# A fused attention and mixture-of-experts kernel: block sums copied into six chunks by DMA instead of VectorE, a third buffer for the values of the sparse part, full-width summary scores, and two more x tiles transposed by DMA

## The chip, the core and the metric

The kernel runs on one core of a Trainium2 chip. The core has five engines that run their own instruction streams in order: TensorE (PE; its weight loads are shown as PEld), VectorE (DVE), ScalarE (ACT), GpSimd (POOL) and SyncE (SP). They meet through semaphores. TensorE writes its results into PSUM banks; everything else lives in SBUF. Transfers are issued by SP and POOL here, each into a queue of its own, and are carried out by the core's 16 DMA engines.

The metric is the device time of one execution in microseconds, the median of several runs. Before the change it is 668.06 us (three runs: 668.44, 667.29, 668.06).

## What is computed

The first part is a sparse attention over q, k, v of shape (4 batches, 8 heads, 768 positions, 64). Each query sees its neighbours closer than 16 positions, and besides them 24 summaries: for each block of 32 positions the maximum of its keys and the mean of its values.

```python
k_sum = k.reshape(B, H, nb, block, D).max(axis=3)
v_sum = v.reshape(B, H, nb, block, D).mean(axis=3)
mask_l = np.abs(pos[:, None] - pos[None, :]) < window
scores_s = scale * np.einsum('bhsd,bhnd->bhsn', q, k_sum) + np.log(block)
a = softmax(concat([where(mask_l, scale * q @ k.T, -1e9), scores_s]))
out = a @ concat([v, v_sum])          # (B, H, S, D)
```

The second part takes that output as x, 3072 tokens of width 512, computes a routing matrix P (3072 by 8) by an exponential and eight rounds of dividing by row and column sums, and adds up eight experts, each `P[:, e] * (relu(x @ w1[e]) @ w2[e])` with a hidden width of 1024.

## The kernel before

**Pairs.** Attention works on 16 pairs of heads, pair `i` holding heads 2(i%4) and 2(i%4)+1 of batch i//4. Pairs 0 to 3 (batch 0) go through `pair_half`, in halves of 384 positions, and start the kernel. Pairs 4 to 15 go through `pair_whole`, six chunks of 128 positions each; the change is about these twelve.

**The steps of a pair from 4 on**, with their names in the planner's table `U`: POOL issues the loads of k, q (two transfers each, L282) and v (L287). TensorE transposes k and q (`tr`, L301; pairs 12 to 15 by DMA on SP instead, L328) and copies go to `kT`, `qT`. VectorE takes the block maxima of k (`ks`, L333) and spreads them by head into `ksT` (`km`, L339). TensorE sums the blocks of v with a constant matrix (`vs`, L355) into PSUM; VectorE scales that into chunk 0 of a value tile `V_e` (L361) and copies it into chunks 1 to 5 (L365); both are the unit `Vs`. SP (pairs 4 to 11) or POOL (12 to 15) copies the rows of v that a chunk's neighbours need into the other half of the partitions of `V_e` (`near`, four small transfers, L375 and L377). TensorE makes the scores in two blocks (`S`, L345), ACT the exponentials, VectorE the masks (L410) and the edge parts in `E_e` (`ed`, L418 and L422). `summaries_2` (`ss`, L459) makes the scores against the summaries, the first half of the positions into PSUM partitions 0 to 63 and the second half into 64 to 127, each with a weight tile of 64 columns; ACT's exponentials of them go into `E_e` (L470). `values` (`A`, L433 and L439) multiplies by v and, with a second group of matmuls, by `V_e`. VectorE normalizes (L540, L541). Last, x is transposed into `xT`: by TensorE into PSUM and a copy (`to_xT`, L548), and for pairs 12 to 14 by a DMA transpose on SP (`x_dma`, L558), as `X_BY_DMA = 12` says; pair 15 goes by TensorE.

**Buffers.** There are `NE = 2` tiles each of `E_e` and `V_e`. So the block sums and the neighbours of pair i wait for the values of pair i-2. POOL writes the constant parts of these tiles once (`value_constants` L694 to L697, `edge_constants` L690), between the load of w2 of expert 0 and the loads of pair 5. There are six buffers for k, q and v.

**The order of the work.** A small list planner (`Plan`) runs when the kernel is built. Each unit has an engine, a cost, dependences, a priority and, for transfers, a lag until the data are taken as landed; the planner picks the earliest startable unit of each engine and so writes each engine's instruction order. On the chip that order is fixed: an engine waits at an instruction until its semaphores are there, whatever stands ready behind it.

**What fills TensorE.** Expert 0 is computed without routing weights, in eight halves of 384 tokens (`hidden0` L209 and `project0` L214), and is slotted between the attention steps as soon as a batch's x is there. Experts 1 to 7 follow; their two products are done by a seven-multiplication scheme on two-by-two blocks (L762, L813). They need their weights, all of x and P.

Of the kernel before, what the change touches and what calls it, by code (L numbers as in the profile page):

```python
# [10 lines left out]
BF16 = mybir.dt.bfloat16  # L11
# [117 lines left out]
def kernel(  # L129
# [30 lines left out]
    BY_DMA = 12  # L160
    X_BY_DMA = 12
    WHOLE = 12
# [56 lines left out]
    NB = PB  # L219
    NE = 2  # L220
    NS = 1
    NA = 3
    stage = ExitStack()
    with tc.manual_schedule():
# [14 lines left out]
        ks = [attn.tile([128, 1, 32], BF16, name=f"ks{i}") for i in range(NB)]  # L239
        ksT = [attn.tile([128, 128], BF16, name=f"ksT{i}") for i in range(NB)]  # L240
        v_x = [attn.tile([128, 2, G, VD], BF16, name=f"vx{i}") for i in range(NQ)]
# [3 lines left out]

        E_e = [attn.tile([128, G, 128], BF16, name=f"Ee{i}") for i in range(NE)]
        V_e = [attn.tile([128, G, 2 * VD], BF16, name=f"Ve{i}") for i in range(NE)]

# [88 lines left out]
        def key_max_split(i):  # L337
            r = i % NB
            nc.vector.tensor_tensor(out=ksT[r][:, 0:64].rearrange("p (j n) -> p j n", j=2),  # L339
                                    in0=ks[r][:].to_broadcast([128, 2, 32]),  # L340
                                    in1=own[:].to_broadcast([128, 2, 32]), op=ALU.mult)
# [16 lines left out]
        def block_out(i):  # L358
            vs = at.pop(("vs", i))[0:64, :].rearrange("p (j d) -> p j d", j=2)
            dst = V_s[i][0:64, :] if i < PB else V_e[i % NE][0:64, 0, :]  # L360
            nc.vector.tensor_tensor(out=dst.rearrange("p (j x) -> p j x", j=2)[:, :, 0:D], in0=vs,  # L361
                                    in1=own_n[:].to_broadcast([64, 2, D]), op=ALU.mult)
            if i >= PB:
                ve = V_e[i % NE]
                nc.vector.tensor_copy(out=ve[0:64, 1:G, :],  # L365
                                      in_=ve[0:64, 0:1, :].to_broadcast([64, G - 1, 2 * VD]))


        def near_values(i):

            sv, ve = v_x[i % NQ], V_e[i % NE]
            eng = nc.sync if i < BY_DMA else nc.gpsimd
            for j in range(2):
                c0, q0 = VD * j, 64 + 32 * j
                eng.dma_start(out=ve[q0 + W:q0 + 2 * W, 1:G, c0:c0 + VD],  # L375
                              in_=sv[128 - W:128, j, 0:G - 1, :])
                eng.dma_start(out=ve[q0:q0 + W, 0:G - 1, c0:c0 + VD],  # L377
                              in_=sv[0:W, j, 1:G, :])
# [48 lines left out]
        def values(i, h):  # L427
            sv, ee, ve, em = v_x[i % NQ], E_e[i % NE], V_e[i % NE], at["em", i]
            av = at["av", i, h] = bank("a", "av")
            for cc in range(HG):  # L430
                c, o = HG * h + cc, cc * 2 * VD
                for j in range(2):
                    nc.tensor.matmul(av[:, o + j * VD:o + (j + 1) * VD],  # L433
                                     lhsT=em[:, j, c, :], rhs=sv[:, j, c, :],
                                     start=(cc == 0 and j == 0), stop=False,
                                     skip_group_check=True)
            for cc in range(HG):
                c, o = HG * h + cc, cc * 2 * VD
                nc.tensor.matmul(av[:, o:o + 2 * VD], lhsT=ee[:, c, :], rhs=ve[:, c, :],  # L439
                                 start=False, stop=True, skip_group_check=True)  # L440

        def summaries(i, h, tag):
            r = i % NB
            ss, rhs = bank(tag, "ss"), qT[r][:, W + h * HS:W + (h + 1) * HS]
            wait_busy("s", i, h, ss)
            at["ss", i, h] = ss
            if i < PB and not h:
                for j in range(2):
                    p = slice(64 * j, 64 * j + 64)
                    nc.tensor.matmul(ss[32 * j:32 * j + 32, 0:HS], lhsT=ks[r][p, 0, :], rhs=rhs[p],  # L450
                                     start=True, stop=True)
                return
            nc.tensor.matmul(ss[:, 0:HS], lhsT=ksT[r][:], rhs=rhs, start=True, stop=True)

        def summaries_2(i):
            r, ss = i % NB, bank("a", "ss")
            for h in range(2):
                at["ss", i, h] = ss[64 * h:64 * h + 64]
                nc.tensor.matmul(ss[64 * h:64 * h + 64, 0:HS], lhsT=ksT[r][:, 0:64],  # L459
                                 rhs=qT[r][:, W + h * HS:W + (h + 1) * HS], start=True, stop=True)  # L460

# [189 lines left out]
        def constants():  # L651
# [10 lines left out]
            for t in ksT:  # L662
                nc.vector.memset(t[:, 64:128], 0.0)
            for t, n in ((own, 64), (own_n, 32)):
# [214 lines left out]
        def pair_start(i, prio):  # L879
# [18 lines left out]
            if i >= PB:  # L898
                U["km", i] = add("DVE", 0.23, lambda: key_max_split(i), [U["ks", i]] + war_q[2:], prio)
            buf = Buffer("a")  # L900
            U["vs", i] = add("PE", 0.4, lambda: block_sums(i),
                             [U["v", i]] + ([U.get(("A", i - NE, 1)), U["vc", i % NE]] if i >= PB else []), prio + 0.01, opens=[buf])
            sc = add("DVE", 0.25, lambda: summary_constants(i), [], prio - 1.0) if 0 < i < PB else None
            U["Vs", i] = add("DVE", 0.28 if i < PB else 0.7, lambda: block_out(i), [U["vs", i], sc],
                             prio + 0.01, uses=[buf])
# [36 lines left out]
        def pair_whole(i, prio):  # L942
            U["near", i] = add("SP" if i < BY_DMA else "POOL", 2.4 if i < BY_DMA else 3.0, lambda: near_values(i),
                               [U["v", i], U.get(("A", i - NE, 1)), U["vc", i % NE]], prio, lag=5.0 if i < BY_DMA else 3.5)
            x1 = []
# [14 lines left out]
            for h in range(2):  # L960
# [4 lines left out]
            buf = Buffer("a")  # L965
            U["ss", i, 0] = U["ss", i, 1] = add("PE", 0.22, lambda: summaries_2(i),
                                                [U["km", i], U["kT", i, 1], U.get(("A", i - NE, 1))], prio, opens=[buf])
            for h in range(2):
                U["sx", i, h] = add("ACT", 0.46, lambda h=h: summary_exp(i, h), [U["ss", i, h]], prio, uses=[buf])
            for h in range(2):  # L970
                buf = Buffer("a")
                U["A", i, h] = add("PE", 0.4, lambda h=h: values(i, h),
                                   [U["mk", i, h], U["ed", i], U["sx", i, h], U["Vs", i], U["near", i]],
                                   prio, opens=[buf])
# [76 lines left out]
        load_pair(PB, "kqv")  # L1051
        load("w2", lambda: load_w2(0), 0.85, 4.0)
        for n in range(NE):
            U["vc", n] = last[0] = add("POOL", 1.2, lambda n=n: value_constants(n), [last[0]])
            U["ec", n] = last[0] = add("POOL", 0.7, lambda n=n: edge_constants(n), [last[0]])
# [36 lines left out]
        def transposed():  # L1092
# [4 lines left out]
            if X_BY_DMA < NP:  # L1097
                nc.gpsimd.tensor_copy(out=warm[:, 4:5], in_=xT[0:32, PB - 2, (B - 1) * S:(B - 1) * S + 1])
            ve = V_e[(NP - 1) % NE]
            for j in range(2):  # L1100
                nc.gpsimd.tensor_copy(out=warm[:, 2 + j:3 + j],
                                      in_=ve[64 + 32 * j:96 + 32 * j, G - 2, VD * j:VD * j + 1])

        last[0] = add("POOL", 0.3, transposed, [last[0], U["near", NP - 1]] + [U["kT", NP - 1, z] for z in range(2)]
                      + [U["x", i] for i in range(X_BY_DMA, NP - 1)])
# [211 lines left out]
```

## Time and profile before

| quantity | value |
|---|---|
| median of three runs | 668.06 us |
| the profiled execution, its own time | 668.44 us |
| its span, first to last instruction | 666.7 us |
| TensorE, VectorE, ScalarE, GpSimd busy | 657.9, 549.2, 410.5, 198.3 us |
| moved by DMA | 67.89 MB in 112,542 packets |
| expert 0's first product with w2 | 34.77 us |
| values of pairs 4, 5, 6, 7, 8, 9 start on TensorE | 40.5, 49.9, 57.2, 63.1, 69.8, 76.5 us |
| values of pairs 10 to 15 start | 83.3, 88.7, 99.3, 105.1, 111.3, 115.4 us |
| first product of expert 1 | 129.47 us |
| last matmuls of expert 0 | about 165 us |

Busy time of each engine by stage, in us of the stage's length:

| stage (us) | PE | DVE | ACT | POOL | GB/s |
|---|---|---|---|---|---|
| 34 to 50 | 15.23 of 16 | 13.30 | 9.76 | 15.50 | 149 |
| 50 to 66 | 16.00 | 15.15 | 11.55 | 15.82 | 145 |
| 66 to 82 | 16.00 | 14.71 | 12.01 | 11.14 | 131 |
| 82 to 98 | 16.00 | 13.39 | 9.95 | 4.27 | 105 |
| 98 to 118 | 20.00 of 20 | 15.42 | 13.32 | 5.67 | 36 |
| 118 to 166 | 48.00 of 48 | 41.47 | 27.51 | 1.18 | 45 |

The table says where each engine is busy, not which one holds up the others. TensorE is busy throughout from 35 us on, and since its ends are modelled, "busy" alone doesn't say that it streams without gaps; for that one looks at the starts of successive matmuls and at the list of its waits.

### The profile page before, as it was taken

Reading aid. Unit: us, or ns where it says so; the run is one execution under the profiler, and the core shown is the slowest. Engines: PE = TensorE matmul, PEld = TensorE weight load, DVE = VectorE, ACT = ScalarE, POOL = GpSimd, SP = SyncE. Lnnn points to the kernel's source line nnn. Section 1 sums busy time; section 2 is a strip of 40 time slices with the busy share of each in tenths; the row PEclk is TensorE's granted clock in tenths of the full one; section 3 lists DMA queues with packets and bytes.
Section 4 is the critical chain, followed back from the end, with each engine's and each line's share of the span. In section 5 each row is a group of like instructions: output and inputs, shape, how many; then the busy total and the mean of one; then the engine's idle time right before and its main releaser. Section 6 shows DMA issues by size and latency. Waiting matters only on the chain.

```text
span 666.7 us, 13260 instructions
## 1 busy us (share of the span) xinstructions
PE 657.9 (99%) x5132; PEld 434.0 (65%) x5132; DVE 549.2 (82%) x1035; ACT 410.5 (62%) x768; POOL 198.3 (30%) x256
## 2 busy tenths in 40 slices
PE   8999999999999999999999999999999999999996
PEld 4656665555676666666666666666666666666665
DVE  7889978799989787888789887888778877988776
ACT  6767766555986566556565665656665656556652
POOL 8899622100132222222221222222122213222123
PEclk9999999999999999999999999999999999999999
DMA  9999992700863647473654656373837465334656
GB/s 168 165 149 145 132 88 43 127 0 1 137 112 64 117 75 116 79 127 64 98 102 76 123 83 106 65 127 61 130 64 130 77 95 95 64 64 112 159 134 198
DMA packets 112542, 67.89 MB, mean 102 GB/s; under 512 B 77920, under 2 KB 90464, under 8 KB 112480
## 3 DMA queue, kind: packets, MB, share of 16 engines
q0 software_dynamic: 94800, 57.46, 65.7%
q1 hardware_dynamic: 17152, 9.58, 6.5%
q8 instruction: 40, 0.66, 0.4%
q14 instruction: 22, 0.18, 0.1%
q10 hardware_dynamic: 528, 0.02, 0.0%
HBM read 52.45 MB, written 6.29 MB: 88 GB/s over the span
## 4 chain that ended last, share of the span: by engine, by line
PE 94%; DMA 3%; POOL 2%; issue 0%; DVE 0%; ACT 0%; POOLq 0%; DVEq 0%
PE yps L813 22%; PE pA L762 22%; PE pY L813 17%; PE pQ L762 11%; PE yps L214 6%; PE hps L209 6%; PE pR L762 5%; DMA w<-in_moe_w_dram 3%; PE sg L345 1%; PE tkq L301 1%; PE av L433 1%; PE vs L355 1%; PE av L439 1%; POOL vx L287 1%; PE tx L548 1%; PE ss L459 1%
## 5 line engine op out<-in xcount | busy, mean ns | idle before, releaser
L813 PEld LDWEIGHTS <-h 128*128 128x128 f16 x2352 | 230.1, 98 | 89.3 <-issue 1.0
L841 POOL DMA_DIRECT2D out_acc<-y x120 | 101.5, 880 | 372.0 <-ACT y L837 97.8
L837 ACT ACTIVATE y<-pY,P_sb 128x256 f32<-128x256 f32 x168 | 79.8, 476 | 124.2 <-PE pY L813 122.5
L828 DVE SCALAR_TENSOR_TENSOR out_acc<-yps,P_sb,out_acc 128x512 f32<-128x512 f32 x128 | 95.2, 744 | 30.2 <-PE yps L813 30.0
L796 DVE TENSOR_TENSOR h<-h 128x1024 f16<-128x1024 f16 x168 | 109.0, 684 | 1.2
L813 PE MATMUL pY<-w,h 128*128 128x256 f16 x672 | 100.2, 273 | 0.6 <-ACT y L837 0.6
L762 PE MATMUL pA<-xT,w 128*128 128x512 f16 x336 | 98.5, 379 | 0.0
L813 PE MATMUL yps<-w2sum,h 128*128 128x256 f16 x672 | 98.1, 273 | 0.0
L813 PE MATMUL yps<-w,h 128*128 128x256 f16 x672 | 93.3, 273 | 0.0
L828 DVE SCALAR_TENSOR_TENSOR out_acc<-pY,P_sb,out_acc 128x512 f32<-128x512 f32 x84 | 62.9, 748 | 29.9 <-PE pY L813 28.2
L762 PEld LDWEIGHTS <-w 128*128 128x128 f16 x672 | 65.8, 98 | 30.9 <-issue 0.2
L762 PEld LDWEIGHTS <-w1sum 128*128 128x128 f16 x504 | 49.3, 98 | 44.2
L784 DVE CUSTOM_DVE_ANT_0 h<-pQ,snap 128x512 f16<-128x512 f32 x84 | 57.6, 685 | 6.0 <-ACT snap L205 3.3
L784 DVE CUSTOM_DVE_ANT_0 h<-pA,snap 128x512 f16<-128x512 f32 x84 | 57.3, 683 | 6.0 <-PE pA L762 5.9
L200 ACT ACTIVATE h<-pA 128x512 f16<-128x512 f32 x84 | 50.6, 603 | 12.4 <-PE pA L762 12.2
L200 ACT ACTIVATE h<-pR 128x512 f16<-128x512 f32 x84 | 50.1, 596 | 7.5 <-PE pR L762 7.4
L205 ACT COPY pR<-pA 128x512 f32<-128x512 f32 x84 | 48.0, 571 | 7.4 <-PE pA L762 6.4
L813 PE MATMUL pY<-w2sum,h 128*128 128x256 f16 x336 | 50.4, 273 | 0.0
L762 PE MATMUL pA<-xsum,w 128*128 128x512 f16 x168 | 50.0, 379 | 0.0
L762 PE MATMUL pQ<-xsum,w1sum 128*128 128x512 f16 x168 | 50.0, 379 | 0.0
L762 PE MATMUL pQ<-xT,w1sum 128*128 128x512 f16 x168 | 50.0, 379 | 0.0
L762 PE MATMUL pA<-xsum,w1sum 128*128 128x512 f16 x168 | 50.0, 379 | 0.0
(149 smaller groups left out, 845.9 us busy)
## 6 DMA issues: line engine op xcount, KB each, us to landing
out_acc<-y POOLq DMA_DIRECT2D x120, 256.0 KB, 3.4
w<-in_moe_w_dram POOLq DMA_DIRECT2D x15, 1024.0 KB, 10.6
out_dram<-out_acc SPq DMA_DIRECT2D x24, 256.0 KB, 2.5
qst<-in_q_dram POOLq DMA_DIRECT2D x32, 96.0 KB, 5.8
vx<-in_v_dram POOLq DMA_DIRECT2D x15, 192.0 KB, 6.6
kst<-in_k_dram POOLq DMA_DIRECT2D x24, 96.0 KB, 6.0
w<-in_moe_w_dram POOLq DMA_DIRECT2D x4, 256.0 KB, 7.9
kst<-in_k_dram POOLq DMA_DIRECT2D x3, 192.0 KB, 4.7
```

Of the source, the lines that this page charges most:

```text
L200: nc.scalar.activation(out=out, in_=in_, func=AF.Relu, bias=0.0, scale=1.0)
L205: (nc.scalar.copy if eng == "ACT" else nc.vector.tensor_copy)(out=out, in_=in_)
L209: nc.tensor.matmul(hp[:, 0:n], lhsT=w1s[e][:, dk, f * 128:(f + 1) * 128], rhs=xT[:, dk, t0:t0 + n], start=(dk == 0), stop=(dk == KD - 1))
L214: nc.tensor.matmul(yp[:, d], lhsT=h[:, f, c * 128:(c + 1) * 128], rhs=w2s[e][:, f, d], start=(f == 0), stop=(f == KF - 1))
L287: nc.gpsimd.dma_start(out=v_x[i % NQ][:].rearrange("p j g x -> p (j g) x")[:, :, 0:D], in_=v[b, h0:h0 + 2].rearrange("j (g p) d -> p (j g) ...
L762: nc.tensor.matmul(dst[:], lhsT=lhsT, rhs=rhs, start=first and k == 0, stop=k == HK - 1, skip_group_check=True)
L784: nc.vector._custom_dve(dve_ops.TENSOR_ADD_SAT, out=ring(e, p, q)[:, q % 2, blk, :], in0=at[src, e, p, q][:], in1=at.pop(("snap", n, e, p, ...
L796: nc.vector.tensor_tensor(out=h[:, :, out_, :], in0=h[:, :, a, :], in1=h[:, :, b, :], op=op)
L813: nc.tensor.matmul(dst[:, d], lhsT=lhsT, rhs=rhs, start=f == 0 and n in (1, 5, 2), stop=f == HF - 1, skip_group_check=True)
L828: nc.vector.scalar_tensor_tensor(out=o, in0=y, scalar=scalar, in1=o, op0=ALU.mult, op1=ALU.add)
L837: nc.scalar.activation(out=at[key][:, d], in_=src, func=AF.Copy, bias=0.0, scale=P_sb[:, t, e:e + 1])
L841: nc.gpsimd.dma_start(out=o, in_=at.pop(("y", e, p, c, key))[:], accum_op=ALU.add)
```

## The change

- `X_BY_DMA` goes from 12 to 9: the x tiles of pairs 9 and 10 are transposed by DMA on SP, too (pair 11 is the last of its batch and stays with TensorE).
- `V_e` gets `NV = 3` tiles in place of two, and POOL writes the constants of three. Block sums and neighbours of pair i now wait for the values of pair i-3. `E_e` stays at two.
- The copy of the block sums into chunks 1 to 5 moves from VectorE to a DMA with a repeated source (`spread_sums`), on SP for pairs 4 to 11 and on POOL for 12 to 15, right behind the four transfers of `near`. `values` depends on it (`U["sp", i]`).
- `ksT` is 192 columns wide, with the 64 columns of the summaries in the middle and zeros around them. `summaries_2` takes a window of 128 columns that starts at 64 or at 0, so each of its two matmuls has full width, and the second one adds to the first in PSUM.
- The planner gets other costs for the units touched, so it writes other orders for all engines between about 37 and 220 us. The order of TensorE up to the summary scores of pair 4 is as before.

```diff
-    X_BY_DMA = 12
+    X_BY_DMA = 9
+    NV = 3
-        ksT = [attn.tile([128, 128], BF16, name=f"ksT{i}") for i in range(NB)]
+        ksT = [attn.tile([128, 192], BF16, name=f"ksT{i}") for i in range(NB)]
-        V_e = [attn.tile([128, G, 2 * VD], BF16, name=f"Ve{i}") for i in range(NE)]
+        V_e = [attn.tile([128, G, 2 * VD], BF16, name=f"Ve{i}") for i in range(NV)]
...
         def block_out(i):
...
-            if i >= PB:
-                ve = V_e[i % NE]
-                nc.vector.tensor_copy(out=ve[0:64, 1:G, :],
-                                      in_=ve[0:64, 0:1, :].to_broadcast([64, G - 1, 2 * VD]))
+        def spread_sums(i):
+            ve = V_e[i % NV]
+            (nc.sync if i < BY_DMA else nc.gpsimd).dma_start(
+                out=ve[0:64, 1:G, :], in_=ve[0:64, 0:1, :].to_broadcast([64, G - 1, 2 * VD]))
...
         def summaries_2(i):
             r, ss = i % NB, bank("a", "ss")
             for h in range(2):
                 at["ss", i, h] = ss[64 * h:64 * h + 64]
-                nc.tensor.matmul(ss[64 * h:64 * h + 64, 0:HS], lhsT=ksT[r][:, 0:64],
-                                 rhs=qT[r][:, W + h * HS:W + (h + 1) * HS], start=True, stop=True)
+                nc.tensor.matmul(ss[:, 0:HS], lhsT=ksT[r][:, 64 - 64 * h:192 - 64 * h],
+                                 rhs=qT[r][:, W + h * HS:W + (h + 1) * HS], start=h == 0, stop=h == 1)
...
             for t in ksT:
-                nc.vector.memset(t[:, 64:128], 0.0)
+                nc.vector.memset(t[:], 0.0)
...
             U["vs", i] = add("PE", 0.4, lambda: block_sums(i),
-                             [U["v", i]] + ([U.get(("A", i - NE, 1)), U["vc", i % NE]] if i >= PB else []), ...
+                             [U["v", i]] + ([U.get(("A", i - NV, 1)), U["vc", i % NV]] if i >= PB else []), ...
-            U["Vs", i] = add("DVE", 0.28 if i < PB else 0.7, lambda: block_out(i), [U["vs", i], sc],
+            U["Vs", i] = add("DVE", 0.28, lambda: block_out(i), [U["vs", i], sc],
...
+            U["sp", i] = add("SP" if i < BY_DMA else "POOL", 0.62 if i < BY_DMA else 0.9, lambda: spread_sums(i),
+                             [U["Vs", i]], prio, lag=5.0 if i < BY_DMA else 3.5)
...
-                                   [U["mk", i, h], U["ed", i], U["sx", i, h], U["Vs", i], U["near", i]],
+                                   [U["mk", i, h], U["ed", i], U["sx", i, h], U["sp", i], U["near", i]],
...
         load("w2", lambda: load_w2(0), 0.85, 4.0)
+        for n in range(NV):
+            U["vc", n] = last[0] = add("POOL", 1.2, lambda n=n: value_constants(n), [last[0]])
         for n in range(NE):
-            U["vc", n] = last[0] = add("POOL", 1.2, lambda n=n: value_constants(n), [last[0]])
             U["ec", n] = last[0] = add("POOL", 0.7, lambda n=n: edge_constants(n), [last[0]])
```

## The prediction

> **What bounds the kernel now.** I read the engine totals first, then the clock in the slices, then the list of TensorE's waits, and last the starts of successive matmuls in the timeline.
>
> ```profile
> PE 657.9 (99%) x5132; PEld 434.0 (65%) x5132; DVE 549.2 (82%) x1035; ACT 410.5 (62%) x768; POOL 198.3 (30%) x256
> PEclk9999999999999999999999999999999999999999
> ```
>
> ```profile
> PE yps L214 <- DMA w<-in_moe_w_dram: 1.3, 1, 1.3
> PE idle L611 <- DVE zeros L630: 1.3, 1, 1.3
> PE pY L813 <- ACT y L837: 0.6, 1, 0.6
> PE tkq L310 <- DMA qst<-in_q_dram: 0.5, 1, 0.5
> PE vs L355 <- DVE vx L205: 0.3, 1, 0.3
> PE hps L209 <- DMA w<-in_moe_w_dram: 0.2, 1, 0.2
> ```
>
> TensorE is the bound, at full clock. Its six waits sum to 4.2 us, and five of them lie before 35 us or at the end; after the wait for w2 at 34.77 us there is none until 660. So a gain counts only as matmul time taken away, and a loss only as a new wait of TensorE. Much of the change concerns VectorE, for which TensorE doesn't wait here.
>
> The timeline of TensorE (start, length, what), the summary scores between other work, and a full-width one:
>
> ```profile
> 34.77 1.02 PE L214 MATMUL yps<-w,h 128*128 128x512 f16 x4 [1.34 <-DMA w<-in_moe_w_dram]
> 36.78 0.35 PE L459 MATMUL ss<-qT,ksT 128*64 128x384 bf16 x2
> ...
> 74.04 0.98 PE L209 MATMUL hps<-xT,w 128*128 128x384 f16 x5
> 74.94 0.35 PE L459 MATMUL ss<-qT,ksT 128*64 128x384 bf16 x2
> 75.23 0.66 PE L209 MATMUL hps<-xT,w 128*128 128x384 f16 x3
> ...
> 23.76 0.34 PE L453 MATMUL ss<-qT,ksT 128*128 128x384 bf16 x1
> 23.93 0.65 PE L209 MATMUL hps<-xT,w 128*128 128x384 f16 x3
> ```
>
> Five hps matmuls follow one another every 0.163 us, so they would be through at 74.85; ss starts at 74.94, and the next hps 0.29 later. The two half-width matmuls run side by side, but going in and out costs extra: 0.38 in all.
>
> The loads, which POOL issues back to back, and what lands late:
>
> ```profile
> 28.54 0.74 POOL L690 MEMSET Ee<- 64x768 bf16 x1
> 29.21 1.65 POOL L282 DMA_DIRECT2D kst<-in_k_dram  x2
> 30.84 1.68 POOL L282 DMA_DIRECT2D qst<-in_q_dram  x2
> 32.46 1.06 POOL L287 DMA_DIRECT2D vx<-in_v_dram  x1
> ```
>
> ```profile
> Ve<-vx SPq DMA_DIRECT2D x32, 10.2 KB, 5.4
> kT<-kst SPq DMA_TRANSPOSE x4, 7.8
> qT<-qst SPq DMA_TRANSPOSE x4, 8.5
> ```
>
> **The change, part by part.**
>
> *x of pairs 9 and 10.* TensorE loses twelve 128-wide transposes. In the timeline six of that width take 0.34 us from first start to the next work. 2 x 0.34 = 0.68 us less. Two copies of 0.55 (DVE) or 0.80 (ACT) go too, off the path. SP gains two DMA transposes, 1.2 to 1.8 us of issue each. In the changed order the one of pair 9 stands between the k/q transposes of pairs 12 and 13, that of pair 10 between k and q of pair 14. Landing 7.8 to 8.5 us after issues near 78.5 and 86 us, x is there by 95; the gate of that batch stands at 98.4 in the new order, expert 0 on it at 103. Hidden.
>
> *Full-width scores.* Two in a row at 0.17 (23.76 to 23.93) are 0.34. Before, a pair takes 0.29, and 0.09 for going in where it doesn't follow the scores, ten times of twelve: 12 x 0.29 + 10 x 0.09 = 4.4, after 12 x 0.34 = 4.1. About 0.3 us less. [...]
>
> So TensorE loses 1.0 us of work.
>
> *The copy on VectorE.* 12 x 0.48 = 5.8 us go (the row of L365), worth nothing by itself: no wait of TensorE after 35 us names VectorE. The planner uses it to bring attention's end forward (the values of pair 15 stand some 4.5 us earlier), but TensorE has the same expert work to do either way. The wider zeroing of ksT adds at most 4 x 0.05 us at 2 us, in front of a 0.88 us wait of VectorE for v; if that cover were gone, 0.2.
>
> *The spreads.* Eight on SP at 0.6 us issue, four on POOL at 0.53. No row shows one: 320 pieces of 260 bytes, against 80 of 130 for a neighbour copy (5.4 us median to landing) and 768 of 256 for a DMA transpose (7.8 to 8.5). Between these ends I take 6. The tightest place is pair 5: neighbours from 40.7 (v landed), spread at 43.2, values near 51.4; 8.2 us are there (8.4 at pair 6, 13 at pair 7), so hidden; at 8.5 TensorE would wait 0.3 us. Queued behind on SP: the neighbours of the next pair and, behind pair 11, the first k/q transposes. These move from 66.7 to about 74, land by 85, and the scores that need them stand at 88. Hidden by 3 us.
>
> *Three value tiles.* POOL writes a third set of constants: one set spans 1.33 us (25.19 to 26.52), ahead of the loads of pair 5 and all later ones. POOL issues these without a pause from 29 us on, so every landing moves by 1.33. And since block sums now wait for pair i-3, the planner puts them earlier on TensorE, by landings that it dates 2 us too early (v of pair 6 is taken for landed at 41.05; the trace has 43.44). I summed the new TensorE order from 34.77 on with the starts-to-starts of the trace (yps 0.216, hps 0.163, six transposes or block sums 0.34, half of the values 0.37, six scores 0.19 plus 0.21 for their switches, the gate 0.61). The same sum over the old order gives 117.4 for x of pair 15, where the trace has 117.67; so I add 0.28. The places in question (TensorE there / landing before / landing 1.33 later):
>
> - k of pair 5: 37.1 / 36.18 / 37.51: waits 0.4
> - v of pair 6: 43.95 / 43.44 / 44.77: 0.8 in all
> - v of pair 7: 48.3 / 47.83 / 49.16: 0.9 in all
> - v of pair 9: 56.5 / 56.65 / 57.98: 1.5 in all
>
> These are not added up, since each wait pushes the next place back; the last one stands for all: 1.5 us. From pair 10 on every load leads by over 4 us. Bounds: were loads not later at all, 0.2 us remain at pair 9. If the DMA engines are full, each spread also pushes the loads back by its 320 pieces at the 1080 a microsecond seen in that stage, 0.3 us; four lie before v of pair 9, so 1.2 more, 2.7.
>
> **Sum.** 668.44 (the profiled execution) - 1.0 + 1.5 = 668.9; the median of the runs lies 0.38 lower, so 668.6, no measurable change. A change is told from none at about 0.2%, 1.3 us.
>
> **Rivals.**
> - *The loads aren't later.* POOL is held twice between 35 and 40 us for 0.2 and 0.4 us; if slots of its queue set the pace, a later start is partly made good. Against it: the issues follow each other at the instruction's own 0.82 us almost everywhere. Price: -1.0 + 0.2, 667.3, and down to 667.0 when nothing waits.
> - *DMA engines full (slower).* For it: loads take 6 us in this stage, 4.6 in the quieter first one, and up to 12.4 from 70 us on, when DMA transposes join. Against it: 6 us stays level from 30 to 65. Decides at v of pair 9 once spreads hold up loads: -1.0 + 2.7, 669.8, from which even the 0.2% is passed.
> - *Spreads or transposes land late.* A spread slower than 8.2 us stops TensorE at the values of pair 5; at 11 us it has waited 3. For it: nothing as large has run on this queue in this stage. Against it: four neighbour copies land 0.6 us apart, as they are issued, so the queue isn't slow by the piece. Price 2 to 4 us: 670 to 672.
> - *It does not do what it says*: the narrow form cheaper than I read it. The rows leave 0.3 us; 668.9, part of the forecast's case.
>
> **How the numbers follow.** Forecast 0.38, with its own range 667.6 to 669.3. Loads not later 0.27: its 667.0 to 667.3 is just inside the bound of 666.7, and the runs spread over 1.1 us, so 0.17 of it counts as faster. DMA full 0.22, late transfers 0.13, both slower. Faster 0.17, same 0.48, slower 0.35. The range takes in the floor less 0.3 for the spread of runs, 666.7, and the first part of the late transfers, 670.6; about 2 in 10 lie outside.
>
> **What would show it.** Right: no L365, ss without 0.09 ahead of it and 0.17 from start to start, and in the list of TensorE's waits new rows tkq and vs behind kst and vx landings between 37 and 58 us, together near 1.5 us. Wrong: TensorE waiting at av L439 for a DMA into Ve (spreads), at sg for kT or qT, or loads of v landing over 7 us after issue; or no new wait at all, and then 667. Any wait of TensorE behind VectorE would show that the earlier order was drawn too tight, which I priced at nothing.

## The result and the profile after

The changed kernel takes 672.0 us (median of six runs, 671.7 to 673.6), the kernel before beside it 667.8 us (six runs, 666.7 to 669.1). The ratio is 1.0067, with a 95% interval of 1.0051 to 1.0082: slower by 0.7%. The forecast was 668.6 us with a range of 666.7 to 670.6. The profiled execution of after took 671.79 us, with a span of 669.8; that of before 668.44 and 666.7. One kernel below, the one with both orders changed, was profiled in an execution at a granted clock of 0.66, so only its other times are used.

TensorE's busy time and the list of its waits in the kernel after (what it waited for, total, times, longest):

```profile
PE 657.3 (98%) x5120; PEld 434.7 (65%) x5120; DVE 545.4 (81%) x1022; ACT 409.7 (61%) x767; POOL 201.9 (30%) x264
```

```profile
PE sg L346 <- DVE qT L205: 2.7, 1, 2.7
PE vs L356 <- DMA vx<-in_v_dram: 1.5, 3, 0.8
PE idle L614 <- DVE zeros L633: 1.3, 1, 1.3
PE tkq L311 <- DMA qst<-in_q_dram: 0.7, 1, 0.7
PE yps L214 <- DMA w<-in_moe_w_dram: 0.6, 1, 0.6
...
PE lp L571 <- ACT xT L205: 0.2, 1, 0.2
PE ss L462 <- DVE ksT L340: 0.2, 1, 0.2
```

Before, nothing stood behind 35 us until 660. Now five waits do: two of the three at vs (0.84 us at 49.11 and 0.38 at 57.83; the third, 0.33, lies at 17.65), lp 0.21, ss 0.17, and one of 2.73 us at the scores, which wait for a copy of VectorE. Together 4.33 us. The first product with w2 starts at 34.83 against 34.77, so what comes before it plays no part. From there to the start of the last matmul the changed kernel takes 630.89 us (to 665.72), the kernel before 627.12 (to 661.89). That is 3.77 more with 4.33 us of waits, so the matmuls themselves got 0.56 us shorter, about half of the 1.0 that was forecast. Behind the start of the last matmul the changed kernel needs 4.07 us against 4.81, which was not forecast. Thus the spans, 669.8 and 666.7, lie 3.1 us apart.

The medians lie 4.2 us apart: the profiled execution of before was 0.7 us above its median, that of after 0.2 below its own. Four of the six runs of after show a mean granted clock of 0.997 instead of 1.000, which the last section comes back to.

The large wait, followed back in the timeline of after (start, length, engine, what; in brackets the idle time before it and what ended it):

```profile
73.93 0.64 SPq L369 DMA_DIRECT2D Ve<-Ve  x1
74.75 1.33 SPq L329 DMA_TRANSPOSE kT<-kst  x1
...
78.87 0.55 DVE L413 TENSOR_TENSOR em<-er,band 128x768 bf16<-128x768 bf16 x1
83.33 0.95 DVE L334 TENSOR_REDUCE ks<-kT 128x24 bf16<-128x768 bf16 x1 [3.92 <-DMA kT<-kst]
84.20 0.55 DVE L205 COPY kT<-tkq 128x768 bf16<-128x768 bf16 x1
84.67 0.55 DVE L205 COPY qT<-tkq 128x768 bf16<-128x768 bf16 x1
...
85.27 0.38 PE L346 MATMUL sg<-qT,kT 64*128 64x160 bf16 x6 [2.73 <-DVE qT L205]
```

Read it upwards. TensorE's scores of pair 11 wait for the qT copy of pair 11. That copy is late because VectorE takes its instructions in a fixed order, and in front of the two copies stands the key maximum of pair 12 (L334), which pair 11 doesn't need. It waits 3.92 us for k of pair 12, whose DMA transpose was issued at 74.75, behind the neighbour copies and the spread of pair 11, and landed at 83.31. In the kernel before the same transpose was issued ahead of the neighbours of pair 10 and landed at 73.73:

```profile
66.71 1.33 SPq L328 DMA_TRANSPOSE kT<-kst  x1
```

### The profile page after: what moved, and what is told of

Its sections match the earlier page's. It is cut to its first block, busy times and chain, and to the rows that moved or that the text cites. A ratio compares the mean times of both kernels' runs of the same rounds, so it can differ in the third digit from the quotient of the medians.

```text
span 669.8 us, 13260 instructions
## 1 busy us (share of the span) xinstructions
PE 657.3 (98%) x5120; PEld 434.7 (65%) x5120; DVE 545.4 (81%) x1022; ACT 409.7 (61%) x767; POOL 201.9 (30%) x264
## 4 chain that ended last, share of the span: by engine, by line
PE 90%; POOL 4%; DMA 4%; DVE 1%; issue 1%; ACT 0%; POOLq 0%; DVEq 0%
PE yps L816 22%; PE pA L765 22%; PE pY L816 16%; PE pQ L765 11%; PE pR L765 5%; PE yps L214 5%; PE hps L209 5%; DMA w<-in_moe_w_dram 1%; DMA kT<-kst 1%; POOL qst L283 1%; POOL vx L288 1%; DMA vx<-in_v_dram 1%; POOL kst L283 1%; PE sg L346 1%; PE av L513 0%
## 5 line engine op out<-in xcount | busy, mean ns | idle before, releaser
L844 POOL DMA_DIRECT2D out_acc<-y x120 | 101.3, 877 | 371.6 <-ACT y L840 102.6
L205 ACT COPY pR<-pA 128x512 f32<-128x512 f32 x80 | 45.6, 570 | 8.9 <-PE pA L765 7.6
L765 PE MATMUL pR<-xT,w 128*128 128x512 f16 x168 | 50.0, 379 | 0.0
```

Of the source, the lines that this page charges most:

```text
L205: (nc.scalar.copy if eng == "ACT" else nc.vector.tensor_copy)(out=out, in_=in_)
L765: nc.tensor.matmul(dst[:], lhsT=lhsT, rhs=rhs, start=first and k == 0, stop=k == HK - 1, skip_group_check=True)
L844: nc.gpsimd.dma_start(out=o, in_=at.pop(("y", e, p, c, key))[:], accum_op=ALU.add)
```

## Two ways to remove the stop

**The key maximum alone moved on VectorE.** In the changed kernel the list of units is edited behind the planner:

```diff
-        for u in plan.order():
+        done = plan.order()
+        u = U["ks", BY_DMA]
+        done.remove(u)
+        done.insert(done.index(U["km", BY_DMA - 1]) + 1, u)
+        for u in done:
```

> Edit: the changed kernel with one VectorE instruction moved: the key maximum of pair 12 stands behind the summary-key split of pair 11 instead of ahead of the kT and qT copies of pair 11. No transfer is issued earlier or later by it. Theory A (VectorE's fixed order: it stands 3.92 us at the key maximum for the DMA transpose of pair 12, and the copies of pair 11 queue behind it): the sg wait of 2.7 us and the ss wait of 0.2 behind it go, about 2.9 us less, 669.1 us; the DMA transposes of pair 12 still land near 83.3. Theory B (the queues and DMA engines are late in this stage, and whichever consumer comes first pays): TensorE waits 2 us or more in this stage at another place, 671.5 to 672.

Measured: 672.4 us, ratio 1.0058 (1.0038 to 1.0078). TensorE's waits in this kernel:

```profile
PE ss L462 <- DVE xs L544: 2.1, 1, 2.1
PE vs L356 <- DMA vx<-in_v_dram: 1.3, 3, 0.6
...
PE ss L462 <- ACT Ee L473: 1.2, 1, 1.2
```

and VectorE in its timeline:

```profile
82.51 0.95 DVE L334 TENSOR_REDUCE ks<-kT 128x24 bf16<-128x768 bf16 x1
...
91.08 0.95 DVE L334 TENSOR_REDUCE ks<-kT 128x24 bf16<-128x768 bf16 x1 [3.40 <-DMA kT<-kst]
```

The sg wait is gone, so VectorE's fixed order did carry the late landing to TensorE; that part of theory A is shown. But one transpose further on the same thing happens: the key maximum of pair 13 waits 3.40 us, as k of that pair took 11.8 us (79.27 to 91.05), and TensorE stands 2.1 and then 1.2 us at the summary scores. The time is that of theory B, and by my estimate about 1.5 us of it come from a half clock: from 94.1 to 97.5 us the granted clock of this profile is 0.50 (see the last section).

**The transposes of pair 12 ahead of the neighbours of pair 11 on SP.**

```diff
+        for z in range(2):
+            u = U["tr", BY_DMA, z]
+            done.remove(u)
+            done.insert(done.index(U["near", BY_DMA - 1]), u)
```

> Edit: the changed kernel with SP's order changed in one place: the k and q DMA transposes of pair 12 stand ahead of the neighbour copies of pair 11 (and so ahead of its spread). Theory A (the position of the transposes on SP behind the neighbours and the spread of pair 11 makes them late, and VectorE's order passes it on): k of pair 12 is issued near 69.7 and lands near 77.7, VectorE reaches its key maximum at 79.3 and doesn't stand; sg and ss waits go, 669.1 us. Price to look for: the neighbours and spread of pair 11 issue 2.5 to 3 us later; the values of pair 11 on TensorE stand late enough to hide that. Theory B (DMA transposes land late because the DMA engines are full from 70 us on): an earlier issue lands hardly earlier, after 81, and at least 1.5 us of the wait stays, 670.6 to 672.

Measured: 669.8 us, ratio 1.0022 (1.0007 to 1.0037). From its timeline:

```profile
68.97 1.78 SPq L329 DMA_TRANSPOSE kT<-kst  x1
...
78.46 0.94 DVE L334 TENSOR_REDUCE ks<-kT 128x24 bf16<-128x768 bf16 x1
79.64 0.56 DVE L205 COPY kT<-tkq 128x768 bf16<-128x768 bf16 x1 [0.25 <-PE tkq L302]
```

k of pair 12 landed at 77.0, VectorE didn't stand, and the wait at sg is gone. Theory A holds here: 2.2 us of the 4.2 by the medians, 3.0 by the ratios, come from where these two transposes stand on SP. A wait of 1.23 us at 92.84, of a summary score for ScalarE's exponential of the one before, and two vs waits of 0.69 and 0.46 us stay.

## The parts of the change one by one

**Full-width scores alone, in the kernel before** (its `ksT` 192 wide, the two matmuls of 128 output rows adding into one bank):

```diff
-                nc.tensor.matmul(ss[64 * h:64 * h + 64, 0:HS], lhsT=ksT[r][:, 0:64],
-                                 rhs=qT[r][:, W + h * HS:W + (h + 1) * HS], start=True, stop=True)
+                nc.tensor.matmul(ss[:, 0:HS], lhsT=ksT[r][:, 64 - 64 * h:192 - 64 * h],
+                                 rhs=qT[r][:, W + h * HS:W + (h + 1) * HS], start=h == 0, stop=h == 1)
```

> Edit: the kernel before with the full-width summary scores alone (wider ksT, two full-width matmuls that add into one bank instead of two half-width ones side by side); the order of the work is that of the kernel before. Theory A (a side-by-side pair costs 0.38 us with going in and out, a full-width pair 0.34): 12 x 0.03 to 0.04 us less, 667.4 us against 667.76. Theory B (the narrow form shares the array and costs less): up to 12 x 0.05 us more, 668.4.

Measured: ratio 0.9991 (0.9976 to 1.0006); the time can't tell the theories apart. The rows of line 459 in the two profiles can: the first and the last of the 24 matmuls start at 36.8 and 107.2 us in the kernel before, 70.4 apart, and here

```profile
L459 PE MATMUL ss<-qT,ksT x24: 323/326/337, 35.2 to 105.3; 128*128 128x384 bf16 x24
```

70.1 apart, 0.3 us less. From the first product with w2 (33.14) to the start of the last matmul (659.83) this kernel takes 626.69 us, 0.43 less than the kernel before. So in the same order the scores save 0.3 to 0.4 us, as forecast.

**x of pairs 9 and 10 by DMA alone, in the kernel before** (line 161).

```diff
-    X_BY_DMA = 12
+    X_BY_DMA = 9
```

> Edit: the kernel before with x of pairs 9 and 10 transposed by DMA, alone; VectorE keeps its copy, the value tiles stay two, and on SP the k and q transposes of pair 12 stay ahead of the neighbour copies of pair 10. Theory A (SP's order behind spreads and neighbours makes the late landing, the x transposes don't): no wait at sg, 12 matmuls of 0.057 less, 667.2 us against 667.87. Theory B (two more DMA transposes among those of pairs 12 to 15 push k of pair 13 back: the transposes land one after another some 2 us apart, and in the run with the key maximum moved k of pair 13 landed at 91.05): TensorE waits 1 to 3 us near 88 to 93, 669 to 671.

Measured: 670.0 us, ratio 1.0035 (1.0022 to 1.0048). Its timeline has one wait behind 36 us:

```profile
94.85 0.70 PE L568 MATMUL lp<-wg_bf,xT 128*128 128x8 f16 x22 [1.99 <-DMA xT<-xs]
```

Theory B's time, by another wait than it named: x of pair 10 was issued at 86.77 and landed at 94.80, and the gate came to it 2 us too early. From the first product with w2 (33.96) to the start of the last matmul (663.04) it takes 1.96 us more than the kernel before, all of it the wait: of the 0.7 us of transposes saved nothing is left in this order. In the changed kernel the wait didn't show: there x of pair 10 landed at 94.89, and TensorE, held up by some 4 us before, came to the gate later.

**x on TensorE again, in the changed kernel.**

```diff
-    X_BY_DMA = 9
+    X_BY_DMA = 12
```

> Edit: the changed kernel with x of pairs 9 to 11 transposed on TensorE as before. SP's order up to the k transpose of pair 12 is that of the changed kernel. Theory A (SP's order alone makes k of pair 12 late): it lands near 83 again and the sg wait stays 2.5 us or more; with 0.7 us of transposes back on TensorE 672 to 673. Theory B (x transposes crowd the queue): the transpose of x of pair 9 is issued behind that of k of pair 12, but if it delays it, k lands by 81 and under 1 us of wait is left, 670 to 671.

Measured: 673.4 us, ratio 1.0087 (1.0075 to 1.0099). Its waits:

```profile
PE sg L346 <- DVE qT L205: 3.3, 1, 3.3
PE vs L356 <- DMA vx<-in_v_dram: 2.1, 2, 1.6
```

k of pair 12, issued at 73.99, landed at 83.49. The x transposes aren't what makes it late; theory A.

**VectorE's copy again, in the changed kernel**; `spread_sums` and its unit go, and the values wait for `block_out`.

```diff
+            if i >= PB:
+                ve = V_e[i % NV]
+                nc.vector.tensor_copy(out=ve[0:64, 1:G, :],
+                                      in_=ve[0:64, 0:1, :].to_broadcast([64, G - 1, 2 * VD]))
...
+            U["sp", i] = U["Vs", i]
```

> Edit: the changed kernel with the block sums spread by VectorE's copy again, as in the kernel before; three value tiles, full-width scores and x by DMA stay. SP has the neighbour copies of pairs 10 and 11 ahead of the k transpose of pair 12 here too. Theory A (the third value tile lets the copies of pair 11 go ahead of that transpose): k of pair 12 is issued after 73 and lands after 81, and TensorE still waits over 1.5 us between 80 and 95, 670.5 to 672. Theory B (the spreads hold SP and the DMA engines): k of pair 12 lands by 79, no wait over 0.5 us there, 668.5 to 669.

Measured: 669.4 us, ratio 1.0029 (1.0015 to 1.0043). k of pair 12 was issued at 72.10 and landed at 78.41, with 6.3 us in flight instead of 8.6, although the neighbours of pair 11 stand ahead of it here too. Counted from the first product with w2 (34.77 us in the kernel before, 34.83 in the changed one, 33.89 here), k of pair 12 lands after 39.0 us in the kernel before, 48.5 in the changed one and 44.5 here. So of the 9.5 us by which the change moved this landing, 4.0 go with the spreads and the order drawn for them; 5.5 stay without them. VectorE's order makes it count. Theory A, by which the third tile alone would bring the whole wait, falls. Theory B's landing came, its time only partly, because another wait appeared. In the timeline of this kernel:

```profile
89.83 0.56 DVE L542 TENSOR_TENSOR xs<-av,rc 128x384 f16<-128x384 f32 x1 [2.66 <-DMA xT<-xs]
...
90.45 0.34 PE L549 MATMUL tx<-ident_x,xs 128*128 128x128 f16 x3 [1.65 <-DVE xs L542]
```

The transpose of x of pair 9 ends at 89.74, 10.7 us after issue, and only then is its source tile free. VectorE has to wait for that tile before it can normalise the next pair.

**Two value tiles in the changed kernel.**

```diff
-    NV = 3
+    NV = 2
```

> Edit: the changed kernel with two value tiles in place of three; block sums by DMA, full-width scores and x by DMA stay. The block sums then wait again for the values two pairs back, and on SP the k transpose of pair 12 comes ahead of the spread of pair 10 and all of pair 11. Theory A (the third tile lets the copies of pair 11 run ahead of the transposes of pair 12, and the block sums ahead of v): neither sg nor vs waits, TensorE's work is 1.0 less than before, 667 to 667.5 us. Theory B (the spreads themselves are what holds SP and the DMA engines): k of pair 12 lands after 79 all the same and TensorE waits over 1.5 us at sg or at the values, 669.5 to 672.

Measured: 676.1 us, ratio 1.0122 (1.0106 to 1.0138). k of pair 12 landed at 81.84 and TensorE waited at the values, as in theory B, but for longer than either theory said. Its waits:

```profile
PE av L442 <- DMA Ve<-vx: 5.0, 1, 5.0
PE av L442 <- DMA Ve<-Ve: 2.0, 2, 1.7
PE vs L356 <- DMA vx<-in_v_dram: 1.7, 2, 1.4
```

The wait of 1.7 us is for the spread of pair 10, which took 8.5 us (76.09 to 84.57). The one of 5.0 us is for the neighbours of pair 11. They were issued from 88.16 on, 9 us after the values of pair 9 had freed their tile, because on SP the transposes of k and q of pair 13 and of x of pair 9 stood ahead of them, and the last landed at 97.02. So in this order the two tiles leave the spread of pair 10 in the open, and the larger loss is SP's order again. That the spreads need a third tile is not shown.

## The order of the work, and what comes back

**Block sums of pairs 7 and 9 later, in the changed kernel.** The copy of the sums on VectorE (`Vs`) follows where it would come too early.

```diff
+        for i, n in ((7, 2), (9, 1)):
+            u, made = U["vs", i], U["Vs", i]
+            pe = [x for x in done if x.on == "PE"]
+            behind = pe[pe.index(u) + n]
+            done.remove(u)
+            done.insert(done.index(behind) + 1, u)
+            if done.index(made) < done.index(u):
+                done.remove(made)
+                done.insert(done.index(u) + 1, made)
```

> Edit: the changed kernel with the block sums of pair 7 two units later on TensorE and those of pair 9 one unit later (and the copy behind them on VectorE), so that other work stands in the places where TensorE waited for v. Theory A (the planner dates these landings too early, and 0.84 us at 49.1 and 0.38 us at 57.8 are lost there for good): both waits go, the sg wait of 2.7 us stays, 670.8 us. Theory B (time lost before the stop at 83 us is given back there, because the DMA transpose that ends it lands at a time of its own): the sg wait grows by the 1.2 us, 671.8 to 672, as before the edit.

Measured: 673.2 us, ratio 1.0069 (1.0049 to 1.0088). Of the vs waits one is left, 0.82 us at pair 9; the sg wait grew to 3.58 us, ended by the landing of k of pair 12 at 82.38. The vs waits are 0.40 us less than in the changed kernel, the stop is 0.85 us longer. Theory B: what was won before the stop was lost in it. More was lost behind it, as the windows show (start and end; length; busy time of PE, PEld, DVE, ACT, POOL with counts; granted clock; DMA share; GB/s):

```profile
82.00:83.00 1.00, 0.00 (x0) 0.00 (x0) 0.60 (x1) 0.00 (x0) 0.00 (x0) 1.00 1.29 109
83.00:84.00 1.00, 0.00 (x0) 0.00 (x0) 1.00 (x3) 0.00 (x0) 0.00 (x0) 0.61 2.24 143
84.00:86.00 2.00, 1.66 (x9) 0.69 (x10) 1.90 (x7) 0.97 (x1) 0.52 (x1) 0.50 1.73 152
...
88.00:90.00 2.00, 2.00 (x12) 0.86 (x12) 1.35 (x4) 1.36 (x3) 0.83 (x3) 0.50 1.71 177
90.00:92.00 2.00, 2.00 (x15) 1.14 (x14) 1.34 (x3) 0.46 (x1) 0.31 (x1) 0.99 1.51 137
```

TensorE's granted clock was 0.50 from 83.2 to 90.0 us. In that time two summary scores (from 88.50 on) take 0.62 us until the next matmul starts, against 0.34 at full clock (from 77.86 on, same run). The stop ended at 84.34, so by an estimate, half of the 5.7 us left, this costs about 2.9 us on top of it. The last section has the stops of the traces and the clock behind them.

**Both order edits together**, the loop over SP's transposes and the loop over the block sums as above.

> Edit: the changed kernel with the transposes of pair 12 ahead of the neighbour copies of pair 11 on SP, and the block sums of pairs 7 and 9 two and one units later on TensorE. Theory A (the waits add up, each with a cause of its own): against the run with the transposes alone moved (669.3 to 669.8) the 0.9 us of vs waits go, the ss wait of 1.2 near 92 stays, 668.7 us. Theory B (what is won at 49 and 58 us is lost again at the next stop): 669.8, with more than 1.8 us at ss or sg.

Measured: 670.2 us, ratio 1.0042 (1.0025 to 1.0059), with a mean clock of 0.995 to 0.997 in three of its runs. That is nearer to theory B, but without a trace the place of the loss stays open.

**The planner told that a DMA transpose lands later**, in the changed kernel.

```diff
-                    U["kT", i, z] = add("DMA", 1.7, None, [U["tr", i, z]], prio, lag=2.0)
+                    U["kT", i, z] = add("DMA", 1.7, None, [U["tr", i, z]], prio, lag=6.0)
...
-                U["x", i] = add("DMA", 1.7, None, [U["xt", i]], prio, lag=2.0)
+                U["x", i] = add("DMA", 1.7, None, [U["xt", i]], prio, lag=6.0)
```

> Edit: the changed kernel with one number of the planner changed: a DMA transpose is dated as landed 6.0 us after its turn on the queue in place of 2.0 (the traces show 7 to 12 us from issue to landing in this stage). The work is the same; SP's order differs in one place, and TensorE and VectorE are given other work while transposes are under way. Theory A (the stops near 83 to 95 us come from an order drawn on landings dated some 5 us too early): the sg wait of 2.7 us goes and none takes its place, TensorE doesn't fall to half clock; the vs waits of 1.2 us stay; 668.5 to 669 us. Theory B (the DMA engines carry more than they can in this stage, and attention's end waits for them whatever the order): over 1.5 us of waits between 75 and 100 us stay at other places, 670 to 672.

Measured: 668.7 us, ratio 1.0016 (1.0005 to 1.0026), 3.3 us under the changed kernel and the lowest of the changed kernel's variants. k of pair 12 still landed at 83.44, but VectorE stood only 0.23 us for it, and TensorE not at all. The waits that stay:

```profile
PE vs L356 <- DMA vx<-in_v_dram: 1.7, 2, 1.1
...
PE av L442 <- DMA Ve<-Ve: 0.6, 1, 0.6
...
PE av L442 <- DMA Ve<-vx: 0.5, 1, 0.5
```

Theory A for the stop; the av waits of 1.1 us at the values of pair 12 are new.

**Loads from pair 4 on dated 2.1 us later as well.**

```diff
-            U[key] = add("LAND", 0, None, [last[1]], lag=0.9)
+            U[key] = add("LAND", 0, None, [last[1]], lag=3.0 if key[0] in "kqv" and key[1] >= PB else 0.9)
```

> Edit: the kernel of the run with the 6.0, and the planner also dates the loads of k, q and v from pair 4 on 2.1 us later. Theory A (all of what the change lost was lost to landings dated too early): the vs waits near 49 and 58 us go as well, TensorE's work is 1.0 us less than before and no wait over 0.5 us stands behind 36 us: 666.9 to 667.5 us, level with before (667.1 to 667.9) or 0.1% under it. Theory B (the third value tile's constants, 1.33 us ahead of the loads, cost time that no order gives back): 1 us or more of vs or tkq waits between 36 and 60 us stay, 668.5.

Measured: 671.1 us, ratio 1.0045 (1.0029 to 1.0061). No vs wait is left, and the tiles' constants weren't the cause that theory B made them. But TensorE, ahead by what it no longer waited, now meets x of pair 10 at the gate:

```profile
PE lp L571 <- DMA xT<-xs: 2.8, 1, 2.8
```

and its granted clock is 0.50 from 95.8 to 102.6 us. Neither theory.

**The remaining waits taken away one by one.** To the kernel with 6.0, block sums of pairs 6 to 9 and the first values of pair 12 are put some units later in TensorE's order, by the loop shown above with other numbers; in the second kernel the numbers are 3, 4, 4 and 6.

```diff
+        for i, n in ((6, 2), (7, 2), (8, 2), (9, 4)):
...
+        u = U["A", BY_DMA, 0]
+        pe = [x for x in done if x.on == "PE"]
+        behind = pe[pe.index(u) + 3]
+        done.remove(u)
+        done.insert(done.index(behind) + 1, u)
```

> Edit: the kernel of the run with the 6.0, and in TensorE's order the block sums of pairs 6, 7 and 8 stand two units later, those of pair 9 four, and the first values of pair 12 three. Theory A (the waits found are the whole loss): of the 2.8 us of vs and av waits in the run with the 6.0 under 0.5 is left, 666.3 us, about 0.2% under the kernel before. Theory B (the stage is bound by its transfers): 1.5 us or more of waits between 36 and 100 us come back at other places, 668 us or more.

> Edit: the same with more room: the block sums of pair 6 three units later, of 7 and 8 four, of pair 9 six, the values of pair 12 three. Theory A: as with less room, 666.3 us, no vs wait at all. Theory B: waits of 1.5 us or more at sg, ss, av or lp between 36 and 100 us, 668 us or more. If later block sums make the spreads late, a new wait of TensorE stands at the values (av) for a DMA into Ve between 48 and 65 us.

Measured: 676.6 and 681.2 us. In these two kernels the block sums of pair 9 (in the second of pairs 7 to 9) fell behind the spread that copies them. The spread sends older sums, so these kernels compute something else, and the block sums then wait for the spread to have read them (6.3 us at one place). The times say nothing on the question. In the next one every spread stays behind its block sums, and pair 9 moves three units.

```diff
+        for i, n in ((6, 2), (7, 2), (8, 2), (9, 3)):
...
+            sent = U["sp", i]
+            if done.index(sent) < done.index(made):
+                done.remove(sent)
+                done.insert(done.index(made) + 1, sent)
```

> Edit: the kernel of the run with the 6.0, and in TensorE's order the block sums of pairs 6, 7 and 8 stand two units later, those of pair 9 three, the first values of pair 12 three; every spread stays behind the block sums that it copies. Theory A (the waits found are the whole loss): of the 2.8 us of vs and av waits in the run with the 6.0 at most 0.5 is left, 666.4 us, about 0.2% under the kernel before. Theory B (the stage is bound by its transfers): 1.5 us or more of waits between 36 and 100 us come back at other places, 668 us or more.

Measured: 668.9 us, ratio 1.0018 (1.0002 to 1.0035). All vs waits are gone, and between 36 and 100 us its timeline has one wait over 0.3 us:

```profile
96.91 0.49 PE L442 MATMUL av<-Ve,Ee 128*128 128x130 bf16 x3 [2.00 <-DMA Ve<-vx]
```

Theory B. The values of pair 12 wait for neighbour copies that POOL had issued from 79.57 on, and the first of these took 15.7 us. 2.8 us of waits are removed, and 2.0 come back where the next transfer is late. Of the matmul time saved nothing shows in this order either: from the first product with w2 (33.36) to the start of the last matmul (662.82) it takes 2.3 us more than the kernel before, with 2.4 us of waits.

**Later dates without spreads and third tile**: the kernel before with the full-width scores and x of pairs 9 and 10 by DMA. The planner dates k and q 6.0 us and x 9.0 us.

```diff
-    X_BY_DMA = 12
+    X_BY_DMA = 9
...
-                    U["kT", i, z] = add("DMA", 1.7, None, [U["tr", i, z]], prio, lag=2.0)
+                    U["kT", i, z] = add("DMA", 1.7, None, [U["tr", i, z]], prio, lag=6.0)
...
-                U["x", i] = add("DMA", 1.7, None, [U["xt", i]], prio, lag=2.0)
+                U["x", i] = add("DMA", 1.7, None, [U["xt", i]], prio, lag=9.0)
```

> Edit: the kernel before with full-width scores and x of pairs 9 and 10 by DMA, two value tiles and VectorE's copy, and the planner dating DMA transposes of k and q as landed 6.0 us and those of x 9.0 us after their turn in place of 2.0. Theory A (each stop between 65 and 100 us is an order drawn on a landing dated too early, so honest dates leave only the 1.0 us of work saved): no wait of TensorE over 0.5 us between 36 and 660 us, 666.7 us, 0.15% under before. Theory B (x by DMA comes too late for the gate of its batch whatever the order, as TensorE has no other work left by then): a wait at lp of 1 us or more stays, 668 to 669.5.

Measured: 675.1 us, ratio 1.0108 (1.0091 to 1.0125). The gate no longer waits, and between 36 and 100 us only 0.99 and 0.20 are lost (vs and tx, behind VectorE). But the planner wrote another order for the experts behind attention too, and there TensorE waits from 148 to 187 us for ScalarE:

```profile
PE pA L762 <- ACT snap L205: 5.6, 5, 1.4
```

So theory B's wait at the gate didn't come, but the time doesn't decide between the theories, and none of the kernels tried is shown to be faster than the kernel before.

## Why the prediction was wrong

*TensorE's work, -1.0 us: right in direction, about half in size.* 0.56 us came, as the accounting at the top shows. The scores' 0.3 was seen in the kernel with them alone, and the transposes left (tx) take 0.60 us less in all, summed from start to start, against the 0.68 forecast. But in the new order other matmuls took part of both back, and with x by DMA alone all of it. The expectations of the runs carried the 1.0 on, so by this their lowest times, 666.3 to 667.5 us, stand about half a microsecond too low.

*Three value tiles, 1.5 us of vs waits: right in mechanism and nearly in size.* 1.22 us came, at pairs 7 and 9; k of pair 5 and v of pair 6, taken to wait 0.4 and 0.8, didn't. The step "every landing moves by 1.33" was too hard: k of pair 5 was issued 1.48 us later (31.51) and landed at 36.20 against 36.18, v of pair 6 was issued 1.31 later and landed at 43.41 against 43.44; v of pair 7 and 9 did move, by 1.24 and 1.13.

*Spreads landing in time: right.* They took 4.5 to 6.4 us in this stage (41.77 to 46.53 for pair 5), and no value of pairs 4 to 11 waited for one.

*x of pairs 9 and 10: hidden, as put there, but not safely.* x of pair 10 landed at 94.89 ("by 95"), and its gate came at 103.56. In the kernel before, with no time lost ahead of the gate, the same transposes cost 2.0 us, and in the run with later loads 2.8.

*The failed step* is the last of the paragraph on the spreads: "These move from 66.7 to about 74, land by 85, and the scores that need them stand at 88. Hidden by 3 us." The issue (74.75) and the flight (8.6 us) came as put there. The consumer was the wrong one. I looked for TensorE's first use of the tile and took the distance to it for slack. The first reader is VectorE's key maximum of pair 12. The planner, which dates the landing 1.7 + 2.0 us after the issue, had put it ahead of the copies of pair 11, so its reader stood there from 79.4 on, 3.9 us early. Two runs show this: with the key maximum behind the copies the sg wait went although k still landed at 82.23, and with the transposes issued 5.8 us earlier it went, too. "Worth nothing by itself: no wait of TensorE after 35 us names VectorE" is the same fault in another sentence: it holds for an engine whose own inputs are in time, and says nothing of one that is made to stand. I had named a wait behind VectorE as what would show it, and had priced it at nothing; it cost 2.9 us with the ss wait behind it, and likely, by my estimate, the lower clock in some runs (a mean of 0.997 in four of six).

*The rivals.* "Spreads or transposes land late", 0.13, had the right time, 670 to 672, but its place was pair 5's values on TensorE. "DMA engines full" put its price at the loads of v; what was late was the stage of the transposes, from 70 us on, of which the text said only that loads take up to 12.4 us there. The chance for slower, 0.35, was too low for a change that adds twelve spreads and two DMA transposes to queues on which flights of 5 to 9 us were in view.

## What to carry to other kernels

When a transfer moves, follow its landing to the first instruction that reads it on any engine, and then down that engine's fixed order to whatever is queued behind; the bound engine's own first use is not the slack. A stage whose transfers are late gives back little of what is saved in it: here seven edits with a trace took away all or part of a wait that they aimed at, and in each one others of 0.9 to 3.3 us opened or grew, in six of them at a late landing. A planner's landing dates are part of the kernel: one number, 2.0 to 6.0, was worth 3.3 us.

## What was not expected of the hardware

A stop of TensorE can cost more than its length. In the run with the block sums of pairs 7 and 9 later, the granted clock was 0.50 until 90.0 us, 5.7 us beyond the end of a stop of 3.58. Ten traces, with their stops of 2.0 us and more behind 36 us (and one of 1.2 close behind another), read as follows:

| kernel | stops of TensorE (us) | granted clock at their end and behind | mean clock of the profiled execution |
|---|---|---|---|
| x by DMA alone | 2.0 | 1.00 | 1.000 |
| the changed kernel | 2.73 | 1.00 | 1.000 |
| every spread behind its sums | 2.0 | 1.00 | 1.000 |
| spreads ahead of their sums, with more room | 6.1 and 4.3 | 0.50, twice for 6.8 us | 0.990 |
| the same with less room | 6.3 | 0.50 for 6.8 us | 0.995 |
| loads dated later, too | 2.8 | 0.50 for 6.8 us | 0.994 |
| block sums of pairs 7 and 9 later | 3.58 | 0.50 for 6.8 us | 0.994 |
| key maximum moved | 2.1 and 1.2 | 0.50 for 3.4 us | 0.997 |
| x on TensorE again | 3.3 | 0.50 for 3.4 us | 0.997 |
| two value tiles | 5.0 | 0.50 for 6.8 us | 0.994 |

In these traces a stop of 2.0 us (twice) and one of 2.73 us left the clock at 1.00, and in the seven others, with one of 2.8 us or more or with 2.1 and 1.2 us close together, it was 0.50 for a while. What sets the lower clock off, and why it lasted 3.4 us in two traces and 6.8 us at a time in the others, is not shown by these runs. In the run with the key maximum moved, six transposes of x take 0.64 us until the next matmul starts at the clock of 0.50 (95.07 to 95.71), against 0.33 at full clock in the run with the block sums later (97.11 to 97.44). So, as an estimate, the lower clock costs half of what is left of it when the stop ends: 1.5 us with the key maximum moved (the stop ends at 94.47, the lower clock at 97.5) to 3.2 us with the loads dated later (96.16 and 102.6).

The mean clock of 0.997 in four of six runs of the changed kernel is that of the changed kernel with x on TensorE, whose trace shows one such stretch, from 85.3 to 88.8 us. The kernel before shows 0.997 in 7 of the 99 runs whose clock is on record. That the stop at sg brings it about in those four runs is likely by my estimate, but they left no trace.

DMA transposes in this stage took 5.7 to 10.6 us in the changed kernel and up to 12.0 in the others. Neighbour copies issued by POOL in the same stretch took up to 11.5 us in the changed kernel and 15.7 in the run with every spread behind its sums. The x transposes behind 100 us took 2.5 to 2.6 us in the changed kernel.
